# The half-filled last K tile of the w_down product as pairs of 64-row products, gathered for four token tiles

## Chip, cores, metric

One core of a Trainium2 chip. The metric is the device time of one execution in microseconds (us), the median of several. Two other measures are used: the *span* (first to last instruction of a profiled execution), and the *stage to the end*, which runs from the start of the first matmul of the stage that was changed to the end of the span. Both come from the start and end times of instructions in the trace.

## The reference

One transformer layer, forward and backward: linear attention with 32 heads on a layer-normed input of 2048 x 640, then a SwiGLU block with F = 1728 hidden columns, and the gradients of the input and of all weights. Only the last product of the forward pass matters here:

```python
def _B_ref(x, w_gate, w_up, w_down):
    g = _silu(x @ w_gate)
    u = x @ w_up
    return (g * u) @ w_down          # (2048 x 1728) @ (1728 x 640)
...
h2 = h + _B_ref(_layernorm(h, axis=-1), B_w_gate, B_w_up, B_w_down)
```

The contraction has 1728 rows, that is 13.5 tiles of 128.

## The kernel before

`m = g * u` is written token-major to a scratch tensor of 14 x 128 = 1792 columns, the last 64 of them zeros. The product stage comes last in the program. It reads `m` back transposed, loads w_down with its missing 64 rows as zeros, and takes the half-filled 14th tile like the others.

```python
# stage 3, after the last group of columns
for c in range(4):
    pool_store(scr_m_v[:, c * 4:(c + 1) * 4, F:FT * P], zpad[:])
...
# transposed loads, MTA = 4 token tiles ahead
def load_mT(t):
    if t % 4 == 0:
        mTs[t // 4] = strips.tile([P, 4, FT, P], BF16, name="mT", tag="S")
    nc.sync.dma_start_transpose(out=mTs[t // 4][:, t % 4], in_=scr_m[t * P:(t + 1) * P, :])
...
wd = big.tile([P, FT, D], BF16, name="wd", tag="B")
nc.sync.dma_start(out=wd[:, :13, :], in_=B_w_down[0:13 * P, :].rearrange("(j p) d -> p j d", p=P))
nc.sync.dma_start(out=wd[:64, 13, :], in_=B_w_down[13 * P:F, :])
nc.vector.memset(wd[64:, 13, :], 0.0)
...
for t in range(ST):                                   # 16 token tiles
    ...                                               # load_mT(t + MTA), load_h1(t + 3)
    ps = mm("ps_o")                                   # one of four PSUM buffers of two banks
    chs = NCH if t < ST - 1 else [(0, 320), (320, 512), (512, 640)]
    for ci, (n0, n1) in enumerate(chs):
        if ci and t == ST - 1:
            ps = mm("ps_o2")                          # last tile: a buffer for each chunk
        po = ps[:, ci % 2, :n1 - n0]
        for j in range(FT):
            nc.tensor.matmul(po, lhsT=mT[:, t % 4, j, :], rhs=wd[:, j, n0:n1],
                             start=(j == 0), stop=(j == FT - 1))
        ...                                           # last tile: add h1 and store by chunk
    ...                                               # else: add h1 (DVE), store
    if t < HG:
        dwo(t)                                        # small weight gradients, one block per tile
    if ST - 1 - DT <= t < ST - 1:
        dwv(t - (ST - 1 - DT))
```

## Time and profile before

| | before |
|---|---|
| time, median of the three executions known then | 823.47 us (822.2 to 824.26) |
| span of the profiled execution | 820.8 us |
| TensorE busy | 99% of the span |
| the ps_o stage, first to last matmul start | 753.54 to 817.70 us |
| stage to the end | 67.22 us |

How to read it: TensorE is the bound, and in the last stage it runs without a gap. The prediction below shows the lines and how they are read.

### The profile page before, as it was taken

What the parts mean: (1) busy time and instruction counts of PE and PEld (TensorE: products, weight loads), DVE (VectorE), ACT (ScalarE), POOL (GpSimd) and SP (SyncE); (2) the same over time, 40 slices, a digit from 0 to 9 for tenths busy, and PEclk for the clock granted to TensorE, in tenths of its full rate; (3) what the DMA queues carried; (4) which work ended last, traced back from release to release, by engine and by line L of the source; (5) the groups of instructions that cost most, each with busy time, mean ns of one, the idle gap of its engine ahead of it and who ended that gap; (6) DMA issues with size and microseconds to landing.
All of it is one profiled execution on the core that took longest, in us unless ns stands there. A gap on an engine that the chain in (4) does not pass through costs nothing.

```text
span 820.8 us, 14051 instructions
## 1 busy us (share of the span) xinstructions
PE 814.0 (99%) x5540; PEld 523.4 (64%) x5540; DVE 443.8 (54%) x875; ACT 291.5 (36%) x412; POOL 187.4 (23%) x345
## 2 busy tenths in 40 slices
PE   8999999999999999999999999999999999999998
PEld 6776656555555555555566677777776777777776
DVE  6888686891087018800760157887884366631222
ACT  6982422770184126400841122323312133322101
POOL 2330022322412412221125301211210121112330
PEclk9999999999999999999999999999999999999999
DMA  9994589998769997894498757985497989899952
GB/s 295 194 351 95 141 183 276 306 203 176 191 127 209 199 220 168 185 246 111 107 244 180 246 141 213 217 209 161 124 235 172 165 162 176 170 185 258 257 155 73
DMA packets 278241, 158.53 MB, mean 193 GB/s; under 512 B 235036, under 2 KB 264797, under 8 KB 278176
## 3 DMA queue, kind: packets, MB, share of 16 engines
q1 hardware_dynamic: 251616, 82.04, 52.7%
q0 software_dynamic: 17744, 64.45, 24.9%
q10 hardware_dynamic: 8816, 11.16, 4.3%
q8 instruction: 43, 0.70, 0.3%
q14 instruction: 22, 0.18, 0.1%
HBM read 47.60 MB, written 53.66 MB: 123 GB/s over the span
## 4 chain that ended last, share of the span: by engine, by line
PE 87%; DVE 6%; ACT 3%; DMA 2%; issue 1%; SPq 1%; POOL 0%; DVEq 0%; ACTq 0%
PE ps_dw L627 21%; PE ps_dhn L109 14%; PE ps_dxn L877 8%; PE ps_o L932 7%; PE pu L563 7%; PE pg L558 7%; PE ps_dwqk L109 5%; PE ps_y L109 3%; PE ps_dp L109 3%; PE ps_dk L109 3%; PE ps_gt L678 3%; PE pdm L385 2%; PE ps_dm L385 2%; DVE st L134 1%; ACT phi_r L308 1%; DMA xr<-in_A_x_dram 1%
## 5 line engine op out<-in xcount | busy, mean ns | idle before, releaser
L109 PE MATMUL ps_dhn<-wgT,cols 128*128 128x320 bf16 x864 | 119.5, 299 | 0.0
L627 PE MATMUL ps_dw<-dd,hn 128*128 128x448 bf16 (+1 forms) x640 | 118.8, 346 | 0.0
L109 PEld LDWEIGHTS <-cols 128*128 128x128 bf16 x864 | 84.5, 98 | 32.9
L627 PEld LDWEIGHTS <-hn 128*128 128x128 bf16 x640 | 62.6, 98 | 54.2
L629 DVE CAST dwev<-ps_dw 128x896 bf16<-128x896 f32 (+3 forms) x12 | 10.9, 907 | 123.2 <-PE ps_dw L627 123.2
L629 ACT CAST dwev<-ps_dw 128x896 bf16<-128x896 f32 (+1 forms) x20 | 17.6, 878 | 157.9 <-PE ps_dw L627 157.9
L592 POOL DMA_DIRECT2D scr_dT<-stg x64 | 34.6, 541 | 168.9 <-DMA stg<-dd 168.0
L147 DVE CUSTOM_DVE_ANT_0 lb_a<-lb_dy,hn 128x640 bf16<-128x640 bf16 x32 | 26.4, 825 | 75.4 <-ACT lb_dy L145 75.4
L563 PE MATMUL pu<-wgu,hnT 128*128 128x448 bf16 (+1 forms) x320 | 63.6, 346 | 0.0
L558 PE MATMUL pg<-wgu,hnT 128*128 128x448 bf16 (+1 forms) x320 | 63.6, 346 | 0.0
L932 PE MATMUL ps_o<-wd,mT 128*128 128x320 bf16 (+2 forms) x462 | 62.8, 295 | 0.0
L627 PE MATMUL ps_dw<-m_s,dh 128*128 128x448 bf16 (+1 forms) x320 | 60.4, 346 | 0.0
L877 PEld LDWEIGHTS <-ring 128*128 128x128 bf16 x480 | 47.0, 98 | 18.2
L932 PEld LDWEIGHTS <-mT 128*128 128x128 bf16 x462 | 44.0, 98 | 16.2 <-issue 0.3
L877 PE MATMUL ps_dxn<-wqkvT,ring 128*128 128x320 bf16 x320 | 51.3, 299 | 0.0
L627 PEld LDWEIGHTS <-dh 128*128 128x128 bf16 x320 | 31.3, 98 | 27.1
L563 PEld LDWEIGHTS <-hnT 128*128 128x128 bf16 x320 | 31.3, 98 | 27.1
L558 PEld LDWEIGHTS <-hnT 128*128 128x128 bf16 x320 | 31.3, 98 | 27.0
L385 PEld LDWEIGHTS <-dh2T 128*128 128x128 bf16 x320 | 31.1, 98 | 25.5 <-issue 0.6
L298 PE MATMUL ps_kq<-wqk,xnT 128*128 128x320 bf16 x320 | 46.4, 299 | 1.0 <-ACT xnT L290 1.0
L385 PE MATMUL ps_dm<-wdT,dh2T 128*128 128x448 bf16 (+1 forms) x240 | 46.9, 344 | 0.3 <-ACT dmst L399 0.2
L145 ACT ACTIVATE lb_dy<-ps_dhn,rstd 128x640 bf16<-128x640 f32 x16 | 12.7, 793 | 87.8 <-PE ps_dhn L109 87.8
(163 smaller groups left out, 1277.5 us busy)
## 6 DMA issues: line engine op xcount, KB each, us to landing
scr_dT<-stg POOLq DMA_DIRECT2D x48, 224.0 KB, 3.2
cols<-scr_dT POOLq DMA_DIRECT2D x6, 1728.0 KB, 8.5
scr_m<-m_s POOLq DMA_DIRECT2D x12, 448.0 KB, 4.5
cols<-scr_dT ACTq DMA_DIRECT2D x2, 1728.0 KB, 9.7
out_dram<-dwev POOLq DMA_DIRECT2D x30, 112.0 KB, 3.0
scr_dT<-stg POOLq DMA_DIRECT2D x16, 192.0 KB, 2.6
scr_pk<-pk SPq DMA_DIRECT2D x4, 640.0 KB, 7.8
scr_pq<-pqa SPq DMA_DIRECT2D x4, 640.0 KB, 8.1
```

The costliest lines, as they stand in the source:

```text
L109: nc.tensor.matmul(ps[:, ci, :320], lhsT=lhs(k), rhs=rhs(k, *NCH[ci]), start=(start and k == 0), stop=(stop and k == n - 1))
L147: nc.vector.tensor_tensor_reduce(out=a[:], in0=dy[:], in1=xhat, scale=1.0, scalar=0.0, op0=ALU.mult, op1=ALU.add, accum_out=sums[:, 1:2])
L298: nc.tensor.matmul(ps[:, ci, :320], lhsT=xnT[:, t, k, :], rhs=wqk[:, k, w0 + n0:w0 + n1], start=(k == 0), stop=(k == DT - 1))
L385: nc.tensor.matmul(ps[:, c, :w], lhsT=dh2T[:, kt, (t + c) * P:(t + c + 1) * P], rhs=wdT[:, kt, o:o + w], start=(kt == 0), stop=(kt == DT - 1))
L558: nc.tensor.matmul(pg[:, c, :w], lhsT=hnT[:, kt, (t + c) * P:(t + c + 1) * P], rhs=wg[:, kt, 0:w], start=(kt == 0), stop=(kt == DT - 1))
L563: nc.tensor.matmul(pu[:, c, :w], lhsT=hnT[:, kt, (t + c) * P:(t + c + 1) * P], rhs=wg[:, kt, w:2 * w], start=(kt == 0), stop=(kt == DT - 1))
L592: nc.gpsimd.dma_start(out=scr_dT[t + c, :, KO[g]:KO[g] + GK[g], :], in_=stg[:, :GK[g], :])
L627: nc.tensor.matmul(ps[:, c, :w], lhsT=lhs(t), rhs=rhs(t), start=(t == 0), stop=(t == ST - 1))
L629: copy(out=ev[:, :len(parts), :w], in_=ps[:, :len(parts), :w])
L678: nc.tensor.matmul(ps[:, ci, :320], lhsT=dh1[:, t, i * P:(i + 1) * P], rhs=pqs_tm[:, t, n0:n1], start=(t == 0), stop=(t == ST - 1))
L877: nc.tensor.matmul(ps[:, ci, :320], lhsT=lhs[:, i, :], rhs=rhs[:, i, n0:n1], start=(k == 0 and i == 0), stop=(k == 2 and i == DT - 1))
L932: nc.tensor.matmul(po, lhsT=mT[:, t % 4, j, :], rhs=wd[:, j, n0:n1], start=(j == 0), stop=(j == FT - 1))
```

## The change

The intent: instead of multiplying 64 rows of zeros, split the array in two halves of 64 rows and let two of the half-filled products run at once, one in each half. For that the 64 rows of w_down and of `m` are put into both halves of their tiles. As changing between the full array and halves costs something, the half products are gathered for up to four token tiles, which is as many as there are PSUM buffers.

```diff
-    MTA = 4
+    MTA = 5
...
-                    pool_store(scr_m_v[:, c * 4:(c + 1) * 4, F:FT * P], zpad[:])
+                    pool_store(scr_m_v[:, c * 4:(c + 1) * 4, F:FT * P], m_s[:, c * 4:(c + 1) * 4, w - 64:w])
...
-        nc.vector.memset(wd[64:, 13, :], 0.0)
+        nc.sync.dma_start(out=wd[64:, 13, :], in_=B_w_down[13 * P:F, :])
...
+        small_of = {2: [(dwo, 0)], 3: [(dwo, 1)], 6: [(dwo, 2), (dwv, 0)], 7: [(dwo, 3), (dwv, 1)],
+                    10: [(dwo, 4), (dwv, 2)], 11: [(dwo, 5), (dwv, 3)], 13: [(dwv, 4)]}
+        halves_at = {1: range(4), 5: range(4, 8), 9: range(8, 12), 12: (12, 13), 14: (14, 15)}
...
+        def po(t, ci):
+            if (t, ci // 2) not in pso:
+                pso[t, ci // 2] = mm("ps_o")
+            n0, n1 = chunks(t)[ci]
+            return pso[t, ci // 2][:, ci % 2, :n1 - n0]
...
+        def part(t, ci, j, h, last):
+            n0, n1 = chunks(t)[ci]
+            r = slice(0, P) if h is None else slice(64 * h, 64 * h + 64)
+            nc.tensor.matmul(po(t, ci), lhsT=mTs[t // 4][r, t % 4, j, :], rhs=wd[r, j, n0:n1],
+                             start=(t, ci) not in opened, stop=last)
+            opened.add((t, ci))
...
+            for ci, (n0, n1) in enumerate(chunks(t)):
+                for j in range(FT - 1):
+                    part(t, ci, j, None, j == FT - 2 and not late)
...
+            if t in halves_at:
+                n = 0
+                for u in halves_at[t]:
+                    for ci in range(len(chunks(u))):
+                        part(u, ci, FT - 1, n % 2, u <= t)
+                        n += 1
+                for u in halves_at[t]:
+                    if u <= t:
+                        finish(u)
```

In the batch behind tile 1, for example, tiles 0 and 1 get their last product and tiles 2 and 3 their first.

More of the change, by code (lines that the diff above doesn't have):

```diff
@@ L917, with chunks, finish @@
             load_h1(t)
+        small_of = {2: [(dwo, 0)], 3: [(dwo, 1)], 6: [(dwo, 2), (dwv, 0)], 7: [(dwo, 3), (dwv, 1)],
+                    10: [(dwo, 4), (dwv, 2)], 11: [(dwo, 5), (dwv, 3)], 13: [(dwv, 4)]}
+        halves_at = {1: range(4), 5: range(4, 8), 9: range(8, 12), 12: (12, 13), 14: (14, 15)}
+        pso = {}
+        def chunks(t):
+            return NCH if t < ST - 1 else [(0, 320), (320, 512), (512, 640)]
+        def po(t, ci):
[3 more added lines that the diff above has]
+            return pso[t, ci // 2][:, ci % 2, :n1 - n0]
+        opened = set()
+        def part(t, ci, j, h, last):
[4 more added lines that the diff above has]
+            opened.add((t, ci))
+        def finish(t):
+            h1r = h1rs.pop(t)
+            if t < ST - 1:
+                nc.vector.tensor_tensor(out=half(h1r[:]), in0=row(pso.pop((t, 0))), in1=half(h1r[:]), op=ALU.add)
+                (nc.gpsimd if t < 10 else nc.scalar).dma_start(out=o0_v[:, t, :], in_=h1r[:])
+            return h1r
         for t in range(ST):
@@ L922 @@
                 load_h1(t + 3)
-            mT = mTs[t // 4]
-            h1r = h1rs.pop(t)
-            ps = mm("ps_o")
-            chs = NCH if t < ST - 1 else [(0, 320), (320, 512), (512, 640)]
-            for ci, (n0, n1) in enumerate(chs):
-                if ci and t == ST - 1:
-                    ps = mm("ps_o2")
-                po = ps[:, ci % 2, :n1 - n0]
-                for j in range(FT):
-                    nc.tensor.matmul(po, lhsT=mT[:, t % 4, j, :], rhs=wd[:, j, n0:n1],
-                                     start=(j == 0), stop=(j == FT - 1))
+            if t == ST - 1:
+                h1r = finish(t)
+            late = t in (0, 1, 4, 5, 8, 9, 12, 14)
+            for ci, (n0, n1) in enumerate(chunks(t)):
+                for j in range(FT - 1):
+                    part(t, ci, j, None, j == FT - 2 and not late)
                 if t == ST - 1:
-                    nc.vector.tensor_tensor(out=h1r[:, n0:n1], in0=po, in1=h1r[:, n0:n1], op=ALU.add)
+                    nc.vector.tensor_tensor(out=h1r[:, n0:n1], in0=po(t, ci), in1=h1r[:, n0:n1], op=ALU.add)
                     (nc.sync, nc.scalar, nc.sync)[ci].dma_start(out=o0_v[:, t, n0:n1], in_=h1r[:, n0:n1])
-            if t < ST - 1:
-                nc.vector.tensor_tensor(out=half(h1r[:]), in0=row(ps), in1=half(h1r[:]), op=ALU.add)
-                (nc.gpsimd if t < 10 else nc.scalar).dma_start(out=o0_v[:, t, :], in_=h1r[:])
-            if t < HG:
-                dwo(t)
-            if ST - 1 - DT <= t < ST - 1:
-                dwv(t - (ST - 1 - DT))
+            if t in halves_at:
[7 more added lines that the diff above has]
+                        finish(u)
+            elif not late and t < ST - 1:
+                finish(t)
+            for f, i in small_of.get(t, ()):
+                f(i)
 _INS = ['A_x', 'A_wqkv', 'A_wo', 'B_x', 'B_w_gate', 'B_w_up', 'B_w_down', 'grad_out']
```

## The prediction

> **What bounds the kernel now.** I read the page's table of busy time first, then the chain that ended last, then that chain in order of time for the stage that the change touches, then the instructions around it. The page begins:
>
> ```profile
> span 820.8 us, 14051 instructions
> PE 814.0 (99%) x5540; PEld 523.4 (64%) x5540; DVE 443.8 (54%) x875; ACT 291.5 (36%) x412; POOL 187.4 (23%) x345
> ```
>
> TensorE is busy in 99% of the span and no other engine passes 54% (weight loads, 64%, run beside the matmuls). So nearly every nanosecond taken from TensorE's stream comes off the end, and nearly every one added goes on. The stage in question is the last one, the w_down product (line 932, tile ps_o). The chain in order of time, from 700 us on, shows it as a row of equal pieces; the columns are start, length, what:
>
> ```profile
> 753.71 3.80 PE ps_o L932 x28
> 757.51 0.27 PE ps_dwo L899 x2
> ...
> 773.81 0.27 PE ps_dwo L899 x2
> 774.08 3.80 PE ps_o L932 x28
> 777.88 0.38 PE ps_dwo L899 x2
> 778.26 19.12 PE ps_o L932 x140
> 797.39 0.29 PE ps_dwv L128 x7
> ```
>
> The reader is to see three things. The pieces touch, so TensorE waits for nothing here. One token tile is 28 matmuls in 3.80 us, so a 128x320 matmul costs 3.80/28 = 0.136 us of the path. (The mean of 299 ns that the page prints for these matmuls is start to end of one; they overlap.) And the seven ps_dwv matmuls, each with its own 128-column weight load, take 0.29 us, 41 ns each: weight loads can follow one another every 41 ns, although one lasts 98 ns.
>
> The line at 777.88 is the clue for this change. Its two matmuls are the block with only 40 output columns. They take 0.38 us where the same pair with 120 columns takes 0.27, and the 140 ps_o matmuls behind take 19.12 us where five pieces of 3.80 make 19.00. Going into a part of the array and coming back therefore cost about 0.11 + 0.12 = 0.23 us. The timeline shows how, in weight loads that were not fetched ahead:
>
> ```profile
> 777.81 0.12 PEld L899 LDWEIGHTS <-mats 128*40 128x40 bf16 x2 [0.27 <-issue]
> 778.19 18.86 PEld L932 LDWEIGHTS <-mT 128*128 128x128 bf16 x140 [0.26 <-issue]
> ```
>
> A second witness is the ps_dz product, whose products use 32 array columns each and go round the four column groups:
>
> ```profile
> 617.09 0.66 PE ps_dz L786 x16
> 617.74 1.55 PE ps_dkvt L484 x30
> 619.29 0.66 PE ps_dz L786 x16
> ```
>
> Sixteen 320-wide products on the full array would be 16 x 0.136 = 2.17 us; they take 0.66. Four at a time is 4 x 0.136 = 0.54, so sharing is nearly perfect and 0.12 us is left for going in. Behind it, 25 matmuls of 120 and 5 of 40 elements take 1.55 us; at the streaming rate that 0.136 us for 320 gives they'd be about 1.4 to 1.45, so coming out is another 0.1 to 0.15. Again some 0.22 us for the round trip.
>
> **What the Trainium skill says.** "TensorEngine Tiling (Array Packing)", Key Properties: changing the tiling mode, not just the tile, drains TensorE. The trace agrees: 0.23 and about 0.22 us per round trip above. The same page, Gotcha 1: different row tiles cannot write one PSUM bank at the same time. Here the two products of a pair are the two 320-column halves of one token tile, which lie in two banks, so that should not bite; no run yet shows it. "TensorE: Matmul & The Clock Gate", Part 3, Measured speedup: four 32-row tiles of 512 columns reached 3.07 of 4. The trace has no row pairs; its column groups reached almost 4 of 4. The same page, LDWEIGHTS: a weight load costs by its columns, not its rows, so a 64-row load is as dear as a full one. The trace can't show that, but at 41 ns per load two fit well into 136.
>
> **The change part by part.** *Removed:* the last K tile has 64 real rows and 64 zero rows. Its matmuls cost as much as full ones: 15 tiles x 2 x 0.136 = 4.07 us, and the last token tile's three chunks of 320, 192 and 128 columns, 0.136 x (640/320) = 0.27. Sum 4.34 us, all on the path.
>
> *Added:* the same 33 products, each of 64 rows, alternating between the upper and lower half of the array. If a pair takes the time of one, the three batches of four token tiles (8 products) take 4 x 0.136 = 0.54 us each, the batch of tiles 12 and 13 takes 0.27, and that of 14 and 15 takes 0.136 + 0.136 + 128/320 x 0.136 = 0.33. Sum 1.63 + 0.27 + 0.33 = 2.23 us. Gross gain 4.34 - 2.23 = 2.1 us.
>
> *Also added:* five batches, five round trips between the full array and its halves, 5 x 0.22 = 1.1 us. Net gain 1.0 us. By batch: three gain 1.09 - 0.54 - 0.22 = 0.33 each, the fourth 0.05, the fifth loses nothing much. So the gathering of four tiles is what makes it pay: tile by tile there would be 16 round trips, 3.5 us, more than the gross gain.
>
> *Moved, off the path:* the second copy of 64 rows of w_down comes by another transfer of 80 KB instead of a DVE memset of 0.33 us. The spare columns of scr_m are filled with the last 64 real columns instead of zeros, in as many stores of the same size. The first token tile is fetched one turn earlier, so five are queued ahead. The program order shows the same number of transposing transfers ahead of the wd load as before. Evictions of tiles 0, 1, 4, 5 and so on wait for their batch; the dwo and dwv blocks move between tiles. Following the four PSUM buffers in program order, every tile opened finds a buffer whose eviction (0.82 us on DVE, 0.69 on ACT) was started at least a whole tile, about 3.5 us, before. The tail stays: the last tile's chunks are only shorter by one matmul each.
>
> **The rivals.** *First: TensorE waits for data at the start of the stage.* The queue of SyncE shows how near that is:
>
> ```profile
> 734.09 0.45 SPq L888 DMA_DIRECT2D wd<-in_B_w_down_dram  x1
> 734.58 2.81 SPq L889 DMA_DIRECT2D wd<-in_B_w_down_dram  x1
> 737.44 8.10 SPq L841 DMA_TRANSPOSE mT<-scr_m  x1
> ```
>
> The view of tile wd gives 11.8 to 12.0 us to landing, so wd is there at 746 to 749, and the first ps_o matmul starts at 753.5. That is 4 to 7 us of slack against one more 80 KB piece, and the last mT transfer is issued at 775.9 for a tile needed at 814. A stall is unlikely; it would add 1 to 4 us.
>
> *Second: the halves don't share the array,* because a 64-row weight load can't go ahead of a running matmul of the same half, or because of PSUM. Then 4.34 us stays and 1.1 us of switching comes on top: 824.6. For it: this trace has no pair of row halves. Against it: the column groups share almost perfectly, with a load for every product.
>
> *Third: sharing works but the round trip is dearer,* as the loads after a switch have 128 columns rather than 40 or 32. At 0.4 us each, five make 2.0 and the gain is gone: 823.4.
>
> *Fourth: the gain is hidden anyway,* because something else ends the stage. The chain speaks against it: it goes through ps_o to 817.9 with no gap, and only DVE's last addition and the store lie behind.
>
> **Range and chances.** Central: 823.47 - 1.0 = 822.5 us. The largest gain, with free switching, would be 2.1 us (821.4), and the rivals reach 824.6, a stall perhaps 827. The three runs before spread from 822.2 to 824.26, so the spread of runs is as large as the effect. I take 820.9 to 824.7. Two per cent would be 16.5 us, which no part of this sum comes near; 1% on each side is left for what I haven't seen.
>
> **What would show it right or wrong.** Right: in the chain of the changed kernel a tile of 26 matmuls takes 26 x 0.136 = 3.53 us, a batch of eight half products about 0.76 us with both switches counted, and the tile groups list them as 64-row products. The five batches are preceded and followed by weight loads that weren't fetched ahead, idle for about 0.26 us. The stage from the first ps_o start to the last shortens from 64.2 to about 63.2 us, and all before it keeps its times within 0.5 us. Wrong if the batch of eight takes 1.1 us or more (no sharing), if TensorE shows idle time that ends with a DMA at the stage's start or with DVE or ACT at a PSUM buffer, or if the dxn stage before has grown through the transfer that was moved into it.

## The result

| | before | changed |
|---|---|---|
| time, median of four executions | 822.98 us (822.2 to 824.26) | 821.91 us (821.6 to 822.73) |
| span | 820.8 us | 820.0 us |
| ps_o, first to last matmul start | 64.16 us | 63.28 us |
| stage to the end | 67.22 us | 66.51 us |

The ratio is 0.9988, with a 95% interval of 0.9974 to 1.0002. A ratio here and below is the one for the runs of the same rounds; it isn't quite the ratio of the medians quoted. The change is the same within 2%, as forecast, and the times alone can't even tell it from nothing. The traces can.

The chain of the changed kernel in order of time, from the start of the stage (start, length, what):

```profile
753.62 11.35 PE ps_o L937 x86
764.97 0.27 PE ps_dwo L899 x2
765.24 3.53 PE ps_o L937 x26
768.77 0.27 PE ps_dwo L899 x2
769.05 11.35 PE ps_o L937 x86
```

A tile is now 26 matmuls in 3.53 us. The piece of 86 is three tiles (78 full products) and one batch of eight half products: 11.35 - 78 x 0.1357 = 0.77 us for the batch with both changes of the array. Eight full products would have taken 1.09.

The groups of TensorE's instructions list the half products (31 of the 33 are 320 columns wide; the numbers behind the bar are us busy, mean ns of one, idle us before). The waits of the stage list the loads that could not be fetched ahead (columns: engine and line, what ended the wait, us in total, times, longest):

```profile
L937 PE MATMUL ps_o<-wd,mT 64*128 64x320 bf16 x31 | 3.0, 299 | 0.0
```

```profile
PEld L937 <- issue: 2.6, 10, 0.3
```

There are ten waits, 0.26 us on average, in the weight loads, one on each side of five batches. The timeline of the weight loads shows one such batch:

```profile
760.61 0.39 PEld L937 LDWEIGHTS <-mT 64*128 64x128 bf16 x8 [0.26 <-issue]
761.26 0.79 PEld L937 LDWEIGHTS <-mT 128*128 128x128 bf16 x7 [0.26 <-issue]
```

Finer still are the starts of single matmuls in the trace. Here they are for the first batch of the changed kernel, in ns after the start of the last full product before it:

```
half products   231 235   378 381   514 516   650 652
next full product   881
```

The two of a pair start 2 to 4 ns apart, and pairs follow each other every 136 ns, as single full products do. From 0 to 881 there are five slots of 136, of which one is the full product itself, so 881 - 5 x 136 = 201 ns are left for going in and coming out. In the batch of tiles 12 and 13 it is 609 - 3 x 136 = 201 ns. The second full product behind a batch is late too: it starts 145 to 147 ns after the first instead of 136, so from steady stream to steady stream the trip costs 0.21 us.

One thing was not forecast, at the end. This is the end of the chain, before and then changed:

```profile
814.08 3.86 PE ps_o L932 x42
817.94 0.02 issue
817.96 0.29 DVE h1r L935
```

```profile
809.14 6.45 PE ps_o L937 x54
815.59 0.02 issue
815.61 1.25 PE ps_o L937 x13
816.86 0.02 issue
816.88 0.36 DVE h1r L960
817.24 0.20 DVEq L1000
```

Before, the last tile's three chunks are done one after another and only the eviction of the smallest, 0.29 us, lies behind the last product. Afterwards the order on TensorE is another: 11 of the 13 products of the 128-column chunk come ahead of the 192-column chunk, and both evictions, 0.36 + 0.20 us of the chain, fall behind the start of the last product. From the first ps_o start to the last, 0.88 us were gained, but only 0.71 arrived at the end of the span.

### The profile page after: what moved, and what is told of

The parts are those of the page before. It is cut to its first block, busy times and chain, and to the rows that moved or that the text cites. A ratio compares the mean times of both kernels' runs of the same rounds, so it can differ in the third digit from the quotient of the medians. Undisturbed runs are those within 1.5% of the kernel's fastest.

```text
span 820.0 us, 14053 instructions
## 1 busy us (share of the span) xinstructions
PE 813.3 (99%) x5540; PEld 521.0 (64%) x5540; DVE 442.9 (54%) x874; ACT 290.9 (35%) x412; POOL 187.6 (23%) x345
## 4 chain that ended last, share of the span: by engine, by line
PE 82%; DVE 9%; ACT 3%; DMA 3%; issue 1%; SPq 1%; ACTq 0%; POOL 0%; DVEq 0%
PE ps_dw L627 21%; PE ps_dhn L109 14%; PE ps_dxn L877 8%; PE ps_o L937 7%; PE ps_dwqk L109 5%; PE pu L563 5%; PE pg L558 5%; PE ps_y L109 3%; PE ps_gt L678 3%; PE ps_dp L109 3%; PE ps_dk L109 3%; PE pdm L385 2%; DMA xr<-in_A_x_dram 2%; PE ps_dm L385 2%; DVE st L134 1%
## 5 line engine op out<-in xcount | busy, mean ns | idle before, releaser
L937 PE MATMUL ps_o<-wd,mT 128*128 128x320 bf16 (+3 forms) x462 | 61.3, 295 | 0.0
L937 PEld LDWEIGHTS <-mT 128*128 128x128 bf16 (+1 forms) x462 | 41.8, 97 | 17.6 <-issue 2.6
```

Source lines behind the costliest of these rows:

```text
L937: nc.tensor.matmul(po(t, ci), lhsT=mTs[t // 4][r, t % 4, j, :], rhs=wd[r, j, n0:n1], start=(t, ci) not in opened, stop=last)
```

## The experiments

All kernels below gave correct results and ran against the kernel before on the same chip in five rounds, e1 to e4 on one chip and e5 to e8 on another. By the times, each is the same as before within 2%; where an interval lies wholly on one side of 1, the text says slower or faster. "Stage to the end" is read from the trace of one execution. It repeats well: 66.51, 66.51 and 66.53 us in the changed kernel, e2 and e8, 67.22 twice for the stage as before (before and e6). What comes ahead of the stage, some 753 us, moves by some tenths between profiled executions (in e5 by 3 us): the changed kernel's own two profiles start the stage at 753.46 and 753.82 us, the kernel before at 753.54.

| run | stage to the end, us | against changed | median time, us | ratio to before (95%) |
|---|---|---|---|---|
| before | 67.22 | +0.71 | | |
| changed (profile of the result) | 66.51 | | 821.91 | 0.9988 (0.9974 to 1.0002) |
| e1_one_half | 68.64 | +2.13 | 824.33 | 1.0021 (1.0007 to 1.0035) |
| e2_blocks | 66.51 | 0.00 | 821.94 | 0.9993 (0.9981 to 1.0006) |
| e3_each_tile | 68.71 | +2.20 | 824.28 | 1.0020 (1.0007 to 1.0032) |
| e4_tail | 66.10 | -0.41 | 821.18 | 0.9986 (0.9974 to 0.9999) |
| e5_last3 | 65.98 | -0.53 | 821.83 | 0.9984 (0.9972 to 0.9996) |
| e6_supply | 67.22 | +0.71 | 822.69 | 0.9998 (0.9986 to 1.0010) |
| e7_gather_full | 67.65 | +1.14 | 823.96 | 1.0012 (1.0000 to 1.0024) |
| e8_changed | 66.53 | +0.02 | 822.08 | 0.9996 (0.9980 to 1.0012) |

The kernel before had a median of 822.53 us beside e1 to e4 and 823.32 us beside e5 to e8.

### e1_one_half: is it the sharing?

```diff
-                        part(u, ci, FT - 1, n % 2, u <= t)
+                        part(u, ci, FT - 1, 0, u <= t)
```

> All 33 half products use the lower 64 rows, so no two can share the array; everything else as in the changed kernel. My theory (sharing of pairs gives the gain): a batch of eight takes 8 x 0.136 + 0.22 = 1.31 us instead of 0.76, the five batches together +2.1 us, so the stage from first to last ps_o takes 65.3 us instead of 63.2 and the kernel is about 2.1 us slower than the changed one, about 1.1 us slower than the one before. Rival (a 64-row product is cheap in itself, sharing plays no part): the same 63.2 us as the changed kernel.

The stage to the end grew by 2.13 us, the stage from first to last start from 63.28 to 65.39 us (65.3 was expected). The timeline of the weight loads shows eight loads spread over 0.93 us where the pairs took 0.39:

```profile
761.03 0.93 PEld L937 LDWEIGHTS <-mT 64*128 64x128 bf16 x8 [0.26 <-issue]
```

The starts are 232, 377, 513, 649, 785, 921, 1057, 1192, so a 64-row product that has no partner costs 136 ns, just as a full one. The gain is the sharing: without it, the change makes the kernel slower than before. The stage to the end is then 1.42 us over the kernel before, not the expected 1.1, as 0.43 us of dear end (e7 below) are in it.

### e2_blocks: does the order within a batch matter?

```diff
-                        part(u, ci, FT - 1, n % 2, u <= t)
+                        part(u, ci, FT - 1, int(n >= len(halves_at[t])), u <= t)
```

> Each batch first does all products of the lower half, then all of the upper, instead of alternating. My theory (only neighbours in the order overlap, since products start in order): only the one pair at the boundary of the two blocks shares, so a batch of eight takes about 7 x 0.136 + 0.22 = 1.17 us, and the stage is about 1.6 us longer than in the changed kernel. Rival (the array's queue reorders freely): no difference from the changed kernel.

My theory fell: there was no difference. That the program really has four products of the lower half and then four of the upper was checked in the built program. Yet on the chip the eight weight loads took as long as in alternation:

```profile
760.81 0.40 PEld L937 LDWEIGHTS <-mT 64*128 64x128 bf16 x8 [0.26 <-issue]
```

and the matmuls start in pairs again:

```
half products   232 245   379 392   515 528   650 664
next full product   892
```

The semaphores tell which is which. The first to start carries the wait for the lower rows of w_down, and is first in the program. The second to start, 13 ns later, carries the wait that opens tile 2 and is the fifth in the program. It starts 134 ns before the one that is second in the program. So each half of the array takes its own products in turn, and a product for the idle half overtakes three that wait for the busy one. How far ahead this reaches was not tried beyond these eight.

### e3_each_tile: what does a round trip cost?

```diff
-        halves_at = {1: range(4), 5: range(4, 8), 9: range(8, 12), 12: (12, 13), 14: (14, 15)}
+        halves_at = {t: (t,) for t in range(14)}
+        halves_at[14] = (14, 15)
...
-            late = t in (0, 1, 4, 5, 8, 9, 12, 14)
+            late = t < ST - 1
```

> Each token tile does its own pair straight after its 26 full products (tiles 14 and 15 together as before): 15 round trips into the half array and back instead of 5, with the same pairs. My theory: 10 more round trips at 0.22 us make the stage 2.2 us longer than the changed kernel's (65.4 us). Rival (a switch is free where the pair shares, and the 0.22 us was something else, such as the 40-column loads): within 0.3 us of the changed kernel. Rival of a dearer trip (0.4 us): 4 us longer.

Ten more trips made the stage to the end 2.20 us longer, 0.22 us each, and the kernel slower than before. From the last full product before a pair to the first behind it the starts give 470 to 474 ns, so 0.20 us more than two slots of 136. The rest is the late second product (0.01 us a trip, see above) and the five dwo blocks of 120 columns that here come straight behind a pair: their two matmuls start 183 ns apart instead of 136. In the chain such a block takes 0.41 us and not 0.27, of which some 0.09 is the way back from the halves:

```profile
753.98 11.53 PE ps_o L938 x84
765.51 0.41 PE ps_dwo L899 x2
```

This also shows that gathering, and not the pairing alone, makes the change pay: against e7 below, which has the same dear end and no halves, pairs without gathering are 1.06 us slower.

### e7_gather_full: the moves without the halves

The changed kernel with the products of the last K tile on the full array, and zeros again in both paddings:

```diff
-                        part(u, ci, FT - 1, n % 2, u <= t)
+                        part(u, ci, FT - 1, None, u <= t)
```

> The changed kernel's order and buffers, but the last K tile as full 128-row products with zero rows again, so no switch and no sharing; the moves alone. Theory: ps_o from first to last start as long as before the change within 0.1 us (the moves cost TensorE nothing), but the end after the last product dearer, as in the changed kernel: first ps_o start to end of the span 0.3 to 0.4 us longer than before (67.5 to 67.6 us). Rival (the dear end comes with the half products): 67.2 us, as before.

The stage to the end took 67.65 us, 0.43 more than before the change. The first to the last start took 64.34 us against 64.16, which is more than the 0.1 us that I allowed, as the end shows:

```profile
810.48 6.46 PE ps_o L937 x55
816.95 0.02 issue
816.97 1.25 PE ps_o L937 x13
818.22 0.02 issue
818.24 0.36 DVE h1r L960
818.60 0.20 DVEq L1000
```

It is the end of the changed kernel again, the same 1.25, 0.36 and 0.20 us, without any half product. So the dear end belongs to the moves.

### e4_tail: which move?

In the helper `po`, chunks 0 and 1 of the last tile share a buffer (`ci // 2`), while before the change each chunk had its own. Chunk 1 then has to wait for the eviction of chunk 0, and the scheduler fills the wait with chunk 2. In the timeline of the changed kernel the eviction of chunk 0 runs from 815.07 to 815.56 us and chunk 1 goes on at 815.61; TensorE has stood still for 0.18 us. The edit gives each chunk a buffer:

```diff
-            if (t, ci // 2) not in pso:
-                pso[t, ci // 2] = mm("ps_o")
+            k = ci if t == ST - 1 else 0
+            if (t, k) not in pso:
+                pso[t, k] = mm("ps_o")
             n0, n1 = chunks(t)[ci]
-            return pso[t, ci // 2][:, ci % 2, :n1 - n0]
+            return pso[t, k][:, ci % 2, :n1 - n0]
```

> The changed kernel, but the three chunks of the last token tile get a PSUM buffer each, as before the change. In the changed kernel the first two chunks share a buffer, so the second chunk's products wait for the first's eviction, the scheduler puts the third chunk ahead and two evictions fall behind the last product; the end after the last product took 3.1 us instead of 2.9. Theory: this gives back 0.2 to 0.3 us at the end, the span falls to about 819.7 us, the ps_o stage stays at 63.2 us. Rival (the end is set by the last store alone): no difference.

The end of its chain:

```profile
808.87 7.65 PE ps_o L938 x69
816.52 0.02 issue
816.55 0.29 DVE h1r L961
```

Only the 0.29 us eviction is left behind the last product, and the stage to the end fell to 66.10 us. That is 0.41 us, more than the 0.2 to 0.3 expected: my estimate counted only the part after the last product, and 0.18 us of it lay within the stage. Against the kernel before the gain is now 67.22 - 66.10 = 1.12 us.

### e6_supply: the earlier fetch alone

```diff
-    MTA = 4
+    MTA = 5
```

in the kernel before.

> The kernel before with only the earlier fetch of the first token tile (five transfers queued ahead instead of four). Theory: transfers are hidden; ps_o stage and span within 0.3 us of before, though wd is issued some 2 us later. Rival (the part of the gain or loss that starts before the stage comes from the moved transfers): the first ps_o start moves by more than 0.3 us.

The stage to the end is 67.22 us, as before to the hundredth, and it starts at 753.26 us. The earlier fetch doesn't enter the result. The second copy of w_down's rows was not run alone; no wait for it shows in the changed kernel's trace. (In the changed kernel the queue does issue w_down later:

```profile
736.52 0.44 SPq L888 DMA_DIRECT2D wd<-in_B_w_down_dram  x1
```

against 734.09 before. With 9.8 to 11.0 us to landing, its three pieces are there by some 750 us, still ahead of the first ps_o matmul at 753.46.)

### e5_last3: a version with one round trip less

The last two batches, of two tiles each, gain next to nothing. This version puts tiles 12, 13 and 14 into one batch at tile 13 and leaves tile 15 in the full array. It also has the repaired buffers.

```diff
-        halves_at = {1: range(4), 5: range(4, 8), 9: range(8, 12), 12: (12, 13), 14: (14, 15)}
+        halves_at = {1: range(4), 5: range(4, 8), 9: range(8, 12), 13: (12, 13, 14)}
...
-            late = t in (0, 1, 4, 5, 8, 9, 12, 14)
+            late = t in (0, 1, 4, 5, 8, 9, 12, 13)
...
+                nj = FT if t == ST - 1 else FT - 1
...
-                    pool_store(scr_m_v[:, c * 4:(c + 1) * 4, F:FT * P], m_s[:, c * 4:(c + 1) * 4, w - 64:w])
+                    n = 4 if c < 3 else 3
+                    pool_store(scr_m_v[:, c * 4:c * 4 + n, F:FT * P], m_s[:, c * 4:c * 4 + n, w - 64:w])
+                pool_store(scr_m_v[:, ST - 1, F:FT * P], zpad[:, 0, :])
```

Tile 15's rows 64 to 127 of the last K tile are zeros again, so that the second copy of w_down's rows meets zeros.

> On top of the kernel with the repaired tail: tiles 12, 13 and 14 in one batch of six half products, and tile 15 in the full array (its spare columns in scr_m zeros again), so four round trips instead of five. With 0.20 us per trip as read from the starts in the changed kernel: the last two batches cost 0.27 + 0.20 + 0.33 + 0.20 = 1.00 us there, here 0.41 + 0.20 + 0.27 = 0.88. Theory: the time from the first ps_o start to the end of the span falls from 66.10 us (repaired tail) to 65.98, against 67.22 before the change. Rival (the trips are not what costs): no shorter, or longer because tile 15 does its zero rows.

It took 65.98 us, as worked out: 0.12 us under e4 and 1.24 us under the kernel before. The profiled execution happened to be a long one (span 822.9 us), with the time lost elsewhere: its first ps_o matmul starts at 756.89 us instead of 753.2 to 753.9. Set against e4 matmul by matmul, it loses 1.6 us in the first 11 us, 1.6 between 117 and 142 us, and 0.5 at 713 us, where a ps_dxn matmul waits for a transfer (ring<-dq). The last falls in the dxn stage, whose growth the prediction named as a sign of being wrong; of all the profiles only this one has such a wait, and its cause was not tested. Both e4 and e5 have an interval that lies below 1. Which of the two is faster the times can't tell; only the trace does.

### e8_changed: the change again

The same kernel, timed in five rounds beside the others.

> The changed kernel itself again, for a timing of five rounds on the chip of the others: first ps_o start to end of the span 66.5 us, 0.7 us under the kernel before; time 0.5 to 1.0 us under before.

The stage to the end was 66.53 us, so it repeats to 0.02. Four of its six executions took 821.7 to 822.2 us and two took 824.24 and 826.19, hence the ratio of 0.9996 with a wide interval, although the medians differ by 1.24 us, more than the 0.5 to 1.0 expected. Executions that take 2 to 4 us more now and then were seen in e5, e6 and e7 too; their cause stays open.

## Why the prediction was right, and where it wasn't

- **The bound and the price of a product.** Right: 0.136 us per 320-wide product on the path, half product or full (e1).
- **Pairs share the array.** Right, and fully: starts 2 to 4 ns apart, one pair per 136 ns. The 3.07 of 4 for row tiles that the prediction quotes was a low guide for this; these pairs reach 2 of 2 apart from the trip. A weight load of 64 rows lasted 94 ns in the trace, one of 128 rows 98, so halving the rows saves almost nothing, as the quoted page says. That the time goes by the columns the trace doesn't bear out: with 128 rows, loads of 32, 40, 120 and 128 columns lasted 96, 98, 133 and 98 ns. The two loads of a pair run at the same time.
- **The round trip.** Read as 0.22 us from the 40-column block and ps_dz, measured 0.20 from start to start, 0.21 with the late second product, and 0.22 in e3. That an unrelated block in the trace of before gives the price of a switch was the step that made the sum possible. The second witness was read with a wrong sum: 25 x 120 + 5 x 40 = 3200 columns make 1.36 us at 0.136 us for 320, not 1.4 to 1.45. The starts in that trace need no sum: where 136 ns are usual, the first product behind the change in comes after 228 ns (ps_dz) or 229 (40-column block), the first behind the change back after 232 or 231. In the changed kernel both take 231. So the rival of a dearer trip, 0.4 us because of loads with 128 columns, fell.
- **The batches.** A batch of eight was put at 0.76 us and took 0.77. Gross 2.12 less five trips of 0.21 gives 1.07 us; from first to last start e4 gains 64.16 - 63.10 = 1.06. The other 0.06 of its 1.12 lie behind the last start.
- **"The tail stays."** This step failed. The end became dearer by 0.43 us (e7), because the new helper lets two chunks of the last tile share a PSUM buffer. I followed the buffers for the tiles that open them, and not for the order in which chunks of one buffer are filled and emptied; I should have asked the program order for the end as well. So 1.1 us of gain became 0.71. That the time landed 0.6 us under the central value all the same (821.91 against 822.5) says little: one more execution of the kernel before moved its own median from 823.47 to 822.98. And that the medians differ by 1.07 us, close to the forecast gain of 1.0, is luck, since the trace shows 0.71.
- **The transfers.** The conclusion was right, the reason given was not. There is one transposing transfer more ahead of w_down in the program, not the same number, and its issue came 2.4 us later. The slack of 4 to 7 us covered it.
- **The stage's other rivals.** No wait of TensorE on a transfer or on a PSUM buffer of a new tile was seen. The only wait of that kind in the changed kernel is the one within the last tile.
- **Gathering.** The forecast that tile by tile would be slower than before held (e3, 824.28 us).
- What stays open: whether two halves that write the same PSUM bank would disturb each other. Every pair here writes two banks, and the other case was not tried.

## What to carry to other kernels

A half-filled K tile can be halved in cost by pairing row halves, but each change between full array and halves cost 0.20 us here, as much as one and a half products of 320 columns; gather at least three or four pairs per change, and look in the trace for a block that already changes the array to learn its price. Pairs need not be neighbours in the program: here a product overtook three others. When a restructured loop allocates accumulators by a formula, check the last tile's buffers by themselves: here a shared buffer cost 0.41 us at the very end, where nothing came behind to hide it.

## What the Trainium skill lacked or had wrong

- "TensorE: Matmul & The Clock Gate", Part 3, What overlaps and what doesn't, says that matmuls are in program order in start and end, with no reordering. In e2_blocks the fifth product in the program started 13 ns after the first and 134 ns before the second, as it was for the idle half of the array. Whether their ends are signalled in order the run doesn't show. The same passage lets a weight load overlap a running matmul only where the row group differs (a paragraph above it on the same page also allows for a background weight buffer). In e1_one_half all products are in one half, each with its own load of 94 ns, and still start every 136 ns: counted from the first half product, the second started at 145 ns, the load behind it at 147 and the third product at 281.
- "TensorEngine Tiling (Array Packing)", Key Properties, names the drain at a change of mode but no cost. Here it is 0.20 us for going in and coming back, 95 ns at the way in (231 ns between starts instead of 136).
- "TensorE: Matmul & The Clock Gate", LDWEIGHTS, puts a load's time in proportion to its columns. The loads of 32, 40, 120 and 128 columns here (96, 98, 133 and 98 ns) are not in proportion.
